# Early token loads on ACT's queue, all four early means on ACT, and a reordered plan, in a fused attention and MLP kernel

## The chip, the core and the metric

The kernel runs on one core of a Trainium2 chip. The core has five engines that run side by side, each with its own queue of instructions: TensorE (PE, matrix products), VectorE (DVE), ScalarE (ACT), GpSimd (POOL) and SyncE (SP, which here only issues transfers). An engine takes its queue in order; a wait at its head holds everything behind it. Transfers between HBM and the on-chip memory SBUF are issued from a queue, here SP's or ACT's, and run on 16 DMA engines. TensorE writes to PSUM, 8 banks of 128 partitions by 2 KB.

The metric is the device time of one execution in microseconds (us), the lower the better. Beside it stands a profile of one execution: when each instruction started, how long it took, and what it waited for.

## What is computed

The input x has 2048 tokens of 640 values. It is normalized by row, and two branches use the result: a linear attention of 32 heads with 20 values each, whose feature map is a softmax of a per-head product and of its negative, and a gated MLP of width 1536. The output is the sum of x and both.

```python
xn = _layernorm(x)                                   # (x - mean) / sqrt(var + 1e-5)
qkv = xn @ wqkv                                      # split to q, k, v: 32 heads x 20
pq = einsum("bhsd,hdf->bhsf", q, w_phi)              # the same for k
phi_q = concatenate([softmax(pq), softmax(-pq)])     # the same for k
kv = einsum("bhsf,bhsd->bhfd", phi_k, v);  z = sum_s phi_k
o = einsum(phi_q, kv) / (einsum(phi_q, z) + 1e-6)
attn = o.reshape(B, S, D) @ wo
mlp = (silu(xn @ w1) * (xn @ w3)) @ w2
return x + attn + mlp
```

All inputs and the output are bf16.

## The kernel before

**Tiles.** The tokens are 16 tiles of 128 (`x_tok[:, t, :]`), the model width 5 chunks of 128, the MLP width 12 chunks. The normalized x is needed transposed (`xnT`), with the width on the partitions, as an operand of every product.

**A planner sets the order.** The kernel is not written as a fixed list. Each operation is recorded with its reads and writes, an engine or a choice of engines, an estimated duration and a level (its priority), and TensorE's work is recorded as units: a group of matmuls with the PSUM banks it needs and the operations that empty them. `_Program.schedule` (L169) then plays the program in a model of the engines: at each step it takes, for each engine, the operation that can start first, or one of a higher level that can start within a small slack, and commits it. The slack for PE units is 0.12 us and for other operations 0.09 us; while the planned time lies below `shaken` it is drawn at random from a short list (PE 0.03 to 0.6 us, others 0.03 to 0.4), from a generator seeded with `SEED`. `emit` (L389) turns the order into one list for each engine, with semaphore waits. So the order of every queue is fixed when the program is built, from the model's times, and the chip then runs each queue in that order with its own times. `late(n, us)` (L584) forbids the operations recorded since n to be planned before a given time.

**Transfers in the plan.** `load` (L641) issues an ordinary transfer, `turn` (L645) a transposing one. In the model all transfers share one line: `commit` adds each one's bytes behind the last, whichever queue it is on.

**The first 24 us.** They run through these names:

- `load_x` (L660) loads token tiles, `load_wv` the value weights `wv` in two parts, `load_wT` (L667) the key weights transposed (`wqkT`), `phi` the small matrices of w_phi (`phi_s`), `load_w13` slices of the MLP weights.
- `ln_stats` (L712): for a tile, two BATCH_NORM_STATS and one aggregation on DVE give mean and variance (`bst`, `mv`); POOL then makes r = (var + eps)^-0.5 with an addition and a power.
- `centre` (L736) makes `xc` = x minus its mean. For a tile marked "ACT" in `CENTRED`, ACT sums the row (`junk`, with an accumulator), and DVE or ACT adds the negative mean; for a tile marked "DVE", DVE subtracts the mean of its own statistics.
- `xc_transpose` (L754; "cT" here) transposes `xc` on PE into PSUM and copies it to `xcT`; `v_first` (L765) multiplies it with `wv` and scales by r while emptying PSUM, so that V of tiles 0 to 3 doesn't wait for the full normalization.
- `ln_apply` (L727) normalizes `x_tok` in place: tiles 0 and 1 on POOL (`POOLED`), tiles 2 and 3 on DVE, the others on DVE or ACT. `xn_transpose` (L779; "xT" here) transposes tiles 0 to 3 on PE into `xnT`; tiles from 4 on are transposed by DMA from SP's queue.
- `block_diag` (L795) makes `BDc`, five products of `phi_s` and a mask `GF` on POOL; its level is 0, the lowest of POOL's early work (normalization 1e5, statistics about 2e5). `fold` (L804) multiplies `wqkT` with `BDc` on PE into `Wkp`, the key weights with the feature matrices folded in. `k_tile` (L859) uses `Wkp` and `xnT`.

After that, PE runs V and K tiles and MLP units (`mlp`, L976) until the sums over all tokens (`kv_sum`, L888) are formed, then the attention units of each token tile (`q_tok`, L934: 20 small matmuls into four banks, two copies by ACT, a chain of small DVE operations, and one product of 1280 elements that frees the banks) between Q and MLP units, and last the output tiles (`out_tile`, L994). While PE has nothing, matmuls of zeros (`filler`, L1019) are put in during the first 12 planned us.

**Who loads what, before.** SP's queue: x tiles 0 and 1, wv chunks 0 and 1, x tiles 2 and 3, five weight transposes, MLP weights and x tiles 8 to 15 and so on. ACT's queue: wv chunks 2 to 4 and phi at the start, x tiles 4 to 7 not before 9 us of plan.

Of the kernel before, what the change touches and what calls it, by code (L numbers as in the profile page):

```python
# [4 lines left out]
ACT = mybir.ActivationFunctionType  # L5
# [27 lines left out]
class _Op:  # L33


    __slots__ = ("ways", "eng", "emit", "raw", "war", "bankd", "succ", "unit", "ismm", "start", "end", "inc", "sem",
                 "clock", "idx", "part", "level", "off", "done", "nbytes", "busy", "left", "name", "deps", "gates", "early", "extra")

    def __init__(self, ways):
        self.ways = ways  # L40
# [26 lines left out]
class _Program:  # L67
# [91 lines left out]
            after = list(after) + [self.unit.mms[-1]]  # L159
        return self.add(o, writes, reads, level, after)  # L160

    def dma(self, eng, emit, writes, reads, nbytes, busy=0.45, level=0.0, after=()):
        o = _Op({eng: (emit, busy, 0.0)})
        o.nbytes = nbytes
        return self.add(o, writes, reads, level, after)


# [1 line left out]
    def schedule(self, start, filler=None, filler_until=0.0, seed=None, shaken=0.0):  # L169
# [12 lines left out]
        for u in self.units:  # L182
            t = 0.0
# [7 lines left out]
            while todo:  # L191
                o = todo.pop()
# [11 lines left out]
                d.gates.append(u)  # L204
        free = dict(start)
        bus = 0.0
        mode = "full"
        owner = [None] * 8
        ready = {e: [] for e in ENGINES}
        ready_u = [u for u in self.units if not u.missing]  # L210
        pool_prev = None
        for o in self.all:
            if not o.ismm and not o.left:
                for e in o.ways:
                    ready[e].append(o)

        def commit(o, e, t):
            nonlocal bus, pool_prev
            o.eng = e
            o.emit, o.busy, dur = o.ways[e]  # L220
            o.start = t
            free[e] = t + o.busy
            if o.nbytes:
                bus = max(bus, t + 0.6) + o.nbytes / 1e3
                o.end = bus + 1.2 + o.extra
            else:
                o.end = t + dur
            o.done = True
            self.ops.append(o)
            if e == "POOL" and not o.nbytes:  # L230
# [63 lines left out]
        left = len(self.all)  # L294
        while left:
            best = None
            pick = None
            if ready_u:
# [4 lines left out]
                for u in ready_u:  # L303
                    extra = MODE if u.mode != mode else 0.0
# [19 lines left out]
            for e in ("ACT", "DVE", "POOL", "SP"):  # L324
                if not ready[e]:
                    continue
                ts = [(max(free[e], op_time(o, e)), o) for o in ready[e]]
                t = min(x[0] for x in ts)
                w = 0.09 if seed is None or t > shaken else rng.choice((0.03, 0.09, 0.09, 0.2, 0.4))
                t, o = min((x for x in ts if x[0] <= t + w), key=lambda x: (-x[1].level, x[1].idx))  # L330
                if len(o.ways) > 1 and o.level > 1.5e6:
                    other = min(max(free[f], op_time(o, f)) + o.ways[f][2] for f in o.ways if f != e)
                    if other < t + o.ways[e][2] - 0.02:
                        ready[e].remove(o)
                        del o.ways[e]
# [7 lines left out]
            t, e, x, k = best  # L343
            if e == "PE":
                t0 = free["PE"]
                if filler is not None and t0 < filler_until and t > t0 + 0.25:
# [3 lines left out]
                    else:  # L350
                        i = None
# [37 lines left out]
    def emit(self, finish):  # L389
# [54 lines left out]
        for o in finish[-4:]:  # L444
            lists["SP"].append(("wait", o.sem[2], o.sem[1]))
        return lists
CENTRED = {0: "ACT", 1: "ACT", 2: "DVE", 3: "DVE"}
POOLED = (0, 1)
SEED = 0
TRIPLES = ((0, 3, 0, 60), (3, 3, 60, 60), (6, 3, 120, 60), (9, 3, 180, 60), (12, 3, 240, 60), (13, 3, 300, 20))  # L450


def bass_parallel_sum__linear_kernel_hedgehog__glu_gated_swiglu__prompt_kernel(
# [13 lines left out]
    P = _Program(nc)  # L467
# [23 lines left out]
    phi_s = new("phi_s", [128, DC, DH], bf)  # L491
# [92 lines left out]
    def late(first, us):  # L584
        for o in P.all[first:]:
            o.early = us

    def sb(*aps):
        return [a for a in aps if hasattr(a, "ap")]
# [42 lines left out]

    queue = {"SP": nc.sync, "ACT": nc.scalar}

    def bus(o, elem):
        n = 1
        for s in o.shape:
            n *= s
        return n * 2 / elem / 16 * max(18.0, 10 + 0.0352 * elem) + 100.0

    def load(o, i, level=0.0, eng="SP", after=()):  # L641
        return P.dma(eng, lambda: queue[eng].dma_start(o, i), sb(o), sb(i), bus(o, 2 * o.shape[-1]), 0.45, level,
                     after)

    def turn(o, i, level=0.0, dram=False):  # L645
        d = P.dma("SP", lambda: nc.sync.dma_start_transpose(o, i), sb(o), sb(i), bus(o, 256),
                  1.31, level)
        d.extra = 1.0 if dram else 0.2
        return d
# [6 lines left out]
    phi_t = A_w_phi.rearrange("h d f -> (h d) f").rearrange("(c p) f -> p c f", p=128)  # L656
# [70 lines left out]
    def ln_apply(t, level):  # L727
        o, m, s, z = x_tok[:, t, :], mv[:, t, 0:1], mv[:, t, 4:5], mv[:, t, 6:7]
        ways = [w_op("DVE", "tensor_scalar", (o, o, m, s, ALU.subtract, ALU.mult), 0.35, 0.44)]
        if t in POOLED:  # L730
            ways = [w_op("POOL", "tensor_scalar", (o, o, m, s, ALU.subtract, ALU.mult), 1.25, 1.3)]
        if t >= 4:
            ways.append(w_act(o, o, ACT.Identity, D, s, z))
        add(ways, [o], [o, m, s, z] if t >= 4 else [o, m, s], None, level)
# [299 lines left out]

    consts()
    lv = 9e5
    load_x(0, 1, lv)
    load_x(1, 2, lv - 1)

    def load_wv(a, b, level, eng):  # L1040
        load(wv[:, a:b, :], wqkv_t[:, a:b, 2 * D:3 * D], level, eng)
    load_wv(0, 2, lv - 2, "SP")
    load_x(2, 3, lv - 3)
    load_wv(2, 5, 2e9, "ACT")
    load_x(3, 4, lv - 4)
    load(phi_s[:], phi_t, 2e9 - 1e3, "ACT")
    for e in range(DC):
        load_wT(1, e, lv - 9 - e)
    load_w13(0, 256, lv - 16)
    n = len(P.all)  # L1050
    load_x(4, 8, 1.9e6, "ACT")
    late(n, 9.0)
    load_w13(256, 512, lv - 20)
    load_x(8, 12, lv - 21)
    load_w13(512, 1024, lv - 22)
# [9 lines left out]
    n = len(P.all)  # L1065
    block_diag(0)
    late(n, 8.0)
    for t in range(4):
        if t in CENTRED:
            centre(t, up - t, CENTRED[t])  # L1070
        ln_apply(t, 1e5 - t)
    for t in range(4):
        if t in CENTRED:
            xc_transpose(t, 6e4 - 10 * t + 15)
        xn_transpose(t, 3e4 - t if t in CENTRED else 6e4 - 10 * t + 15)
    for t in range(4, T, 2):
# [18 lines left out]
    n = len(P.all)  # L1095
# [8 lines left out]
    for b in range(3):  # L1104
        for fc in range(FC):
            n = 12 * b + fc
# [6 lines left out]
    for b in range(NB):  # L1113
        for j in range(4):
            t = 4 * b + j
# [4 lines left out]
    for t in range(T):  # L1120
        out_tile(t, when(200 + 5 * t))

    P.schedule({"PE": 1.25, "ACT": 2.1, "DVE": 0.93, "POOL": 0.8, "SP": 0.81}, filler, 12.0, SEED, 25.0)

    lists = P.emit(finish)

# [58 lines left out]
```

The softmax here doesn't subtract the row's maximum and nothing guards it: scores larger than these inputs give would overflow.

## Time and profile before

| | |
|---|---|
| runs (3) | 276.48, 276.58, 276.74 us; median 276.58 |
| profiled execution | 276.66 us, of which the profile's span is 274.9 |
| PE busy | 266.7 us (97%), 2078 matmuls |
| DVE, ACT, POOL busy | 183.1 (67%), 102.6 (37%), 65.7 us (24%) |
| DMA | 21.98 MB, mean 80 GB/s |
| chain that ended last | PE 91%, POOL 3%, ACT 2%, DVE 1%, waits for issue 1%, DMA 1% |
| TensorE's clock | full (1.00) throughout |

The span reaches from the first to the last recorded instruction. "Chain that ended last" follows the work back from the last instruction, at each step to what released it. A busy share is an average over the whole span; the first 16 us differ from the rest, and they are what most of the change touches.

Landing times of the first transfers, from issue: x tile 0 2.3 us; wv chunks 2 to 4 (480 KB, ACT, issued at 1.26) 4.2 us; wv chunks 0 and 1 (320 KB, SP, issued at 1.73) 5.0 us; phi (ACT, issued at 1.75) 5.2 us; x tiles 4 to 7 (640 KB, ACT, issued at 8.41) 4.9 us; the weight transposes 3.6 to 5.9 us.

### The profile page before, as it was taken

The page shows a single profiled execution, that of the slowest core. Times are in us where ns is not written, and L with a number is a line of the kernel's source. Part 1 is how long each engine was busy: PE and PEld are TensorE (multiplying, and loading weights), DVE is VectorE, ACT ScalarE, POOL GpSimd, SP SyncE. Part 2 cuts the span into 40 slices and gives each one's busy share as a digit, 9 for nine tenths or more (in the row PEclk, how much of TensorE's full clock was granted, in tenths as well). Part 3 has the DMA queues.
Part 4 walks back from the last instruction along what each step waited for, and adds up shares of the span by engine and source line. Part 5 has one row for each costly group of instructions (what it writes and reads, how often), then busy time and mean ns, then how long its engine had stood idle before and what let it go on. Part 6 is the DMA issues. An engine that isn't in the chain of part 4 may idle for free.

```text
span 274.9 us, 5053 instructions
## 1 busy us (share of the span) xinstructions
PE 266.7 (97%) x2078; PEld 158.9 (58%) x2097; DVE 183.1 (67%) x319; ACT 102.6 (37%) x187; POOL 65.7 (24%) x103
## 2 busy tenths in 40 slices
PE   6799999999999999999999999999999999999996
PEld 3575477656654447544444445677777774444774
DVE  4698989999957433678978978577661215666112
ACT  6379377564553451256673382010000002222000
POOL 5923556999997000000000000000000000000000
PEclk9999999999999999999999999999999999999999
DMA  7999997910000000803211111243332222000001
GB/s 216 237 317 347 195 132 129 187 67 0 2 0 2 0 0 2 284 6 27 47 26 24 38 36 24 75 99 95 97 96 75 72 72 74 0 0 0 26 24 48
DMA packets 41255, 21.98 MB, mean 80 GB/s; under 512 B 27024, under 2 KB 41232, under 8 KB 41232
## 3 DMA queue, kind: packets, MB, share of 16 engines
q1 hardware_dynamic: 39648, 20.49, 31.2%
q10 hardware_dynamic: 1584, 1.17, 1.5%
q8 instruction: 16, 0.26, 0.4%
q14 instruction: 7, 0.06, 0.1%
HBM read 12.81 MB, written 2.62 MB: 56 GB/s over the span
## 4 chain that ended last, share of the span: by engine, by line
PE 91%; POOL 3%; ACT 2%; DVE 1%; issue 1%; DMA 1%
PE PS L572 91%; POOL x_tok L580 2%; ACT EqT L580 2%; DMA x_tok<-in_A_x_dram 1%; POOL mv L580 1%; PE PS L787 0%; DVE bst L580 0%; DVE hT L580 0%; DVE den_s L580 0%; DVE xres L580 0%; ACT e_s L580 0%; DVE xc L580 0%; PE PS L757 0%; DVE t L580 0%; DVE pr_s L580 0%
## 5 line engine op out<-in xcount | busy, mean ns | idle before, releaser
L572 PE MATMUL PS<-xnT,w_s 128*128 128x512 bf16 x465 | 105.6, 379 | 1.4 <-issue 0.5
L572 PEld LDWEIGHTS PS<-xnT,w_s 128*128 128x128 bf16 x480 | 46.4, 98 | 54.5 <-DVE hT L580 0.8
L572 PE MATMUL PS<-w_s,hT 128*128 128x320 bf16 x384 | 55.0, 299 | 0.0
L580 ACT ACTIVATE th<-PS 128x512 f32<-128x512 f32 x48 | 28.7, 599 | 66.0 <-PE PS L572 66.0
L580 DVE SCALAR_TENSOR_TENSOR t<-th,PS 128x512 bf16<-128x512 f32 x48 | 32.6, 679 | 24.0 <-ACT th L580 23.9
L572 PEld LDWEIGHTS PS<-w_s,hT 128*128 128x128 bf16 x384 | 37.1, 98 | 14.9
L580 DVE TENSOR_TENSOR xres<-PS,xres 128x640 bf16<-128x640 f32 (+1 forms) x17 | 13.4, 786 | 41.2 <-PE PS L572 41.2
L580 POOL TENSOR_TENSOR ekt<-ekt,rS 128x640 bf16<-128x640 bf16 x32 | 39.6, 1275 | 1.5 <-DVE rS L580 1.5
L580 DVE SCALAR_TENSOR_TENSOR hT<-t,PS 128x512 bf16<-128x512 bf16 x48 | 32.5, 677 | 1.3 <-PE PS L572 0.3
L580 ACT ACTIVATE EqT<-PS 128x512 bf16<-128x512 f32 x40 | 21.9, 594 | 12.6 <-PE PS L572 12.6
L580 DVE TENSOR_REDUCE S<-ekt 128x64 f32<-128x1280 bf16 x16 | 22.9, 1458 | 3.4 <-ACT ekt L580 3.4
L572 PE MATMUL PS<-wo_s,oT 128*128 128x320 bf16 x160 | 24.5, 299 | 0.0
L580 DVE TENSOR_TENSOR prod<-PS,g_s 128x1280 bf16<-128x1280 f32 x16 | 23.8, 1490 | 0.5
L580 ACT ACTIVATE ekt<-PS 128x640 bf16<-128x640 f32 x32 | 20.8, 701 | 8.6 <-PE PS L572 8.4
L572 PE MATMUL PS<-Wkp,xnT 128*128 128x320 bf16 x160 | 23.9, 299 | 0.0
L572 PE MATMUL PS<-xnT,Wqp 128*128 128x512 bf16 x96 | 23.1, 380 | 0.3 <-issue 0.2
L580 ACT ACTIVATE e_s<-PS 128x64 f32<-128x64 f32 x32 | 9.1, 284 | 37.6 <-PE PS L572 37.1
L572 PEld LDWEIGHTS PS<-wo_s,oT 128*128 128x128 bf16 x160 | 15.7, 98 | 6.1
L572 PEld LDWEIGHTS PS<-Wkp,xnT 128*128 128x128 bf16 x160 | 15.5, 98 | 6.0
L572 PE MATMUL PS<-wv,xnT 128*128 128x320 bf16 x120 | 18.3, 299 | 0.0
L580 DVE BATCH_NORM_STATS2 bst<-x_tok 128x6 f32<-128x320 bf16 x32 | 14.3, 469 | 3.0 <-DMA x_tok<-in_A_x_dram 3.0
L572 PEld LDWEIGHTS PS<-xnT,Wqp 128*128 128x128 bf16 x100 | 9.3, 98 | 10.8
(68 smaller groups left out, 172.1 us busy)
## 6 DMA issues: line engine op xcount, KB each, us to landing
w_s<-in_B_w_dram SPq DMA_DIRECT2D x4, 640.0 KB, 9.2
xres<-in_A_x_dram SPq DMA_DIRECT2D x16, 160.0 KB, 2.2
out_dram<-xres SPq DMA_DIRECT2D x15, 160.0 KB, 1.8
w_s<-in_B_w_dram SPq DMA_DIRECT2D x1, 1920.0 KB, 9.2
w_s<-in_B_w_dram SPq DMA_DIRECT2D x4, 320.0 KB, 5.5
x_tok<-in_A_x_dram SPq DMA_DIRECT2D x2, 640.0 KB, 8.4
wo_s<-in_A_wo_dram SPq DMA_DIRECT2D x1, 800.0 KB, 4.9
x_tok<-in_A_x_dram SPq DMA_DIRECT2D x4, 160.0 KB, 4.0
```

What stands on the lines that cost most here:

```text
L572: return nc.tensor.matmul(o(u.k), l, r, start=start, stop=stop, skip_group_check=shared)
L580: return getattr(e, name)(*[at(a, u) for a in args], **{k: at(v, u) for k, v in kw.items()})
```

## The change

- Token tile 0 stays on SP's queue. Tiles 1, 2 and 3 are issued from ACT's queue, not before 1.3, 3.3 and 4.3 us of plan, with a level above ACT's other work but one; tiles 4 to 7 stay on ACT's queue, not before 11.3 instead of 9.0.
- wv is issued from SP in three parts (chunks 0 and 1, 2, 3 and 4), phi from SP after the second weight transpose.
- All four of tiles 0 to 3 get their mean from ACT (`CENTRED`).
- The planner's model of transfers takes turns between the two queues, and lets ACT issue a transfer while its last operation is still running (`issue`).
- `SEED` is 433 instead of 0, the random slack acts until 175 us of plan instead of 25, and ACT's start in the plan is 1.12 instead of 2.1. So the order of units and operations is drawn anew over most of the kernel.

What is computed stays the same, and so do the operations other than the means of tiles 2 and 3.

```diff
@@ schedule
+        issue = {"ACT": start["ACT"]}
+        queues = {"SP": [], "ACT": []}
...
+        def transfer(now):
+            nonlocal bus
+            at = dict.fromkeys(queues, 0)
+            left = {q: [o.nbytes for o in v] for q, v in queues.items()}
...
+                turn = sum(queues[q][at[q]].each for q in go)
+                steps = min(left[q][at[q]] for q in go)
...
         def commit(o, e, t):
...
-            free[e] = t + o.busy
+            free[e] = max(free[e], t + o.busy)
+            if e == "ACT":
+                issue[e] = t + (o.busy if o.nbytes else 0.06)
             if o.nbytes:
-                bus = max(bus, t + 0.6) + o.nbytes / 1e3
-                o.end = bus + 1.2 + o.extra
+                o.begin, o.end = t + 0.6, 1e9
+                queues[e].append(o)
+                transfer(t)
...
-                ts = [(max(free[e], op_time(o, e)), o) for o in ready[e]]
+                ts = [(max(issue[e] if o.nbytes and e == "ACT" else free[e], op_time(o, e)), o) for o in ready[e]]
...
-CENTRED = {0: "ACT", 1: "ACT", 2: "DVE", 3: "DVE"}
+CENTRED = {0: "ACT", 1: "ACT", 2: "ACT", 3: "ACT"}
 POOLED = (0, 1)
-SEED = 0
+SEED = 433
...
+    def on_act(a, b, us):
+        n = len(P.all)
+        load_x(a, b, 2e9, "ACT")
+        late(n, us)
     load_x(0, 1, lv)
-    load_x(1, 2, lv - 1)
+    on_act(1, 2, 1.3)
...
     load_wv(0, 2, lv - 2, "SP")
-    load_x(2, 3, lv - 3)
-    load_wv(2, 5, 2e9, "ACT")
-    load_x(3, 4, lv - 4)
-    load(phi_s[:], phi_t, 2e9 - 1e3, "ACT")
+    load_wv(2, 3, lv - 4, "SP")
+    on_act(2, 3, 3.3)
+    load_wv(3, 5, lv - 5, "SP")
+    on_act(3, 4, 4.3)
     for e in range(DC):
         load_wT(1, e, lv - 9 - e)
+        if e == 1:
+            load(phi_s[:], phi_t, lv - 10.5)
     load_w13(0, 256, lv - 16)
-    n = len(P.all)
-    load_x(4, 8, 1.9e6, "ACT")
-    late(n, 9.0)
+    on_act(4, 8, 11.3)
...
-    P.schedule({"PE": 1.25, "ACT": 2.1, "DVE": 0.93, "POOL": 0.8, "SP": 0.81}, filler, 12.0, SEED, 25.0)
+    P.schedule({"PE": 1.25, "ACT": 1.12, "DVE": 0.93, "POOL": 0.8, "SP": 0.81}, filler, 12.0, SEED, 175.0)
```

More of the change, by code (lines that the diff above doesn't have):

```diff
@@ L36 @@
     __slots__ = ("ways", "eng", "emit", "raw", "war", "bankd", "succ", "unit", "ismm", "start", "end", "inc", "sem",
-                 "clock", "idx", "part", "level", "off", "done", "nbytes", "busy", "left", "name", "deps", "gates", "early", "extra")
+                 "clock", "idx", "part", "level", "off", "done", "nbytes", "busy", "left", "name", "deps", "gates", "early", "extra",
+                 "begin", "each")
     def __init__(self, ways):
@@ L160, in op, with dma @@
         return self.add(o, writes, reads, level, after)
-    def dma(self, eng, emit, writes, reads, nbytes, busy=0.45, level=0.0, after=()):
+    def dma(self, eng, emit, writes, reads, pieces, each, busy=0.45, level=0.0, after=()):
         o = _Op({eng: (emit, busy, 0.0)})
-        o.nbytes = nbytes
+        o.nbytes, o.each = pieces, each
         return self.add(o, writes, reads, level, after)
@@ L215, in schedule @@
                     ready[e].append(o)
+        def transfer(now):
+            nonlocal bus
+            at = dict.fromkeys(queues, 0)
+            left = {q: [o.nbytes for o in v] for q, v in queues.items()}
+            t = 0.0
+            bus = 0.0
+            while True:
+                go, wake = [], 1e9
+                for q, v in queues.items():
+                    if at[q] < len(v):
+                        o = v[at[q]]
+                        if o.begin <= t + 1e-9:
+                            go.append(q)
+                        else:
+                            wake = min(wake, o.begin)
+                if not go:
+                    if wake > 1e8:
+                        break
+                    t = wake
+                    continue
+                turn = sum(queues[q][at[q]].each for q in go)
+                steps = min(left[q][at[q]] for q in go)
+                if wake < t + steps * turn:
+                    steps = (wake - t) / turn
+                t += steps * turn
+                for q in go:
+                    left[q][at[q]] -= steps
+                    if left[q][at[q]] < 1e-6:
+                        o = queues[q][at[q]]
+                        e = t + 1.3 + o.extra
+                        if e > now:
+                            o.end = e
+                        at[q] += 1
+                bus = t
+            for q, v in queues.items():
+                while len(v) > 1 and v[0].end < now - 5.0 and v[1].begin < now - 5.0:
+                    v.pop(0)
         def commit(o, e, t):
-            nonlocal bus, pool_prev
+            nonlocal pool_prev
             o.eng = e
@@ L633, in bass_parallel_sum__linear_kernel_hedgehog__glu_gated_swiglu__prompt_kernel, with pieces @@
     queue = {"SP": nc.sync, "ACT": nc.scalar}
-    def bus(o, elem):
+    def pieces(o, elem):
         n = 1
@@ L638, in bus @@
             n *= s
-        return n * 2 / elem / 16 * max(18.0, 10 + 0.0352 * elem) + 100.0
+        return n * 2 / elem / 16, max(18.0, 10 + 0.0352 * elem) / 1e3
     def load(o, i, level=0.0, eng="SP", after=()):
-        return P.dma(eng, lambda: queue[eng].dma_start(o, i), sb(o), sb(i), bus(o, 2 * o.shape[-1]), 0.45, level,
+        return P.dma(eng, lambda: queue[eng].dma_start(o, i), sb(o), sb(i), *pieces(o, 2 * o.shape[-1]), 0.45, level,
                      after)
     def turn(o, i, level=0.0, dram=False):
-        d = P.dma("SP", lambda: nc.sync.dma_start_transpose(o, i), sb(o), sb(i), bus(o, 256),
+        d = P.dma("SP", lambda: nc.sync.dma_start_transpose(o, i), sb(o), sb(i), *pieces(o, 256),
                   1.31, level)
```

## The prediction

> **What bounds the kernel now.** I read the page's busy shares first, then the chain that ended last, then the timeline of the first 20 us by engine, because the diff touches loads and row means that are all spent by then.
>
> The first view is a table of stretches: from to, length, then busy time and (xcount) of PE, PE's weight loads, DVE, ACT, POOL, then clock, DMA share and GB/s.
>
> ```profile
> 4.00:6.00 2.00, 1.60 (x20) 1.05 (x18) 1.62 (x6) 1.21 (x3) 1.24 (x3) 1.00 1.14 350
> 6.00:8.00 2.00, 1.42 (x14) 0.97 (x12) 0.84 (x4) 0.70 (x1) 2.00 (x1) 1.00 1.18 256
> 8.00:10.00 2.00, 2.00 (x21) 1.54 (x20) 1.90 (x7) 1.03 (x2) 1.92 (x5) 1.00 0.93 188
> 10.00:12.00 2.00, 0.36 (x8) 0.19 (x6) 1.19 (x3) 0.56 (x1) 2.00 (x2) 1.00 1.00 273
> 12.00:14.00 2.00, 2.00 (x22) 1.58 (x23) 1.12 (x3) 0.70 (x1) 2.00 (x5) 1.00 1.18 264
> ```
>
> TensorE loses time in 4 to 12 us and, from 12 us on, hardly any: over the windows from 12 to 250 us I count 1.7 us idle, and most of that is pieces of 0.05 and 0.16 us at which the neighbouring group has 9, 19 or 29 of its 10, 20 or 30 matmuls, so a missing record. The only real wait there is 0.29 us at 144.0 (<-DVE hT). POOL has 2.00 of 2.00 us in three of these windows and 1.92 in the fourth.
>
> The second view is the chain of waits, in order of time:
>
> ```profile
> 4.57 0.25 POOL mv L580
> ...
> 5.74 2.53 POOL x_tok L580
> 8.28 0.22 POOL mv L580
> ...
> 9.36 2.53 POOL x_tok L580
> 11.88 0.05 issue
> 11.93 0.45 PE PS L787 x5
> ...
> 15.94 7.27 PE PS L572 x70
> ```
>
> From 4.57 to 11.88 the end is set by POOL; after that by PE's own row of work.
>
> The third is the timeline (start, duration, engine, line, operation, tiles, count, idle before):
>
> ```profile
> 6.85 2.88 PE L572 MATMUL PS<-wv,xcT 128*128 128x320 bf16 x20 [0.58 <-ACT xcT L580]
> 7.36 0.50 DVE L580 BATCH_NORM_STATS2 bst<-x_tok 128x6 f32<-128x320 bf16 x1 [1.16 <-DMA x_tok<-in_A_x_dram]
> 11.93 0.45 PE L787 MATMUL PS<-ident,x_tok 128*128 128x128 bf16 x5 [1.64 <-POOL x_tok L580]
> 12.82 0.44 DVE L580 TENSOR_SCALAR x_tok<-x_tok,mv 128x640 bf16<-128x640 bf16 x1
> 13.66 1.59 POOL L580 TENSOR_TENSOR BDc<-phi_s,GF 128x140 bf16<-128x140 bf16 x4
> 13.72 1.71 DVE L580 TENSOR_SCALAR x_tok<-x_tok,mv 128x640 bf16<-128x640 bf16 x1 [0.46 <-POOL mv L580]
> 15.21 0.73 PE L787 MATMUL PS<-ident,x_tok 128*128 128x128 bf16 x10
> 15.78 1.87 PE L572 MATMUL PS<-BDc,wqkT 128*128 128x140 bf16 x30
> ```
>
> Read here: V0 and V1 start at 6.85, when wv's first half has just landed (issued at 1.73, 5.0 us to landing); tile 2's statistics wait for its DMA until 7.36; PE's fifth transpose set waits 1.64 us for POOL's second normalization; and the folds of Wkp start at 15.78, half a microsecond after POOL's last product BDc (15.25) and after the two last transposes. All products in BDc must be there before a fold, and K0 needs the folds.
>
> **What the Trainium skill says.** "DMA: Bandwidth & Descriptors", section Issuing engines are not separate DMA queues: transfers from any engine run on the same 16 DMA engines and interleave, so a second issuing engine saves issue time only. Its section Queues, rings and completion order adds that each DMA engine takes turns between queues. The trace agrees so far: x tile 0 took 2.3 us alone, wv's 320 KB behind two tiles and beside ACT's 480 KB took 5.0. "SBUF — State Buffer", section SBUF: two separate sides: VectorE in a two-port mode and GpSimd hold a common port pair exclusively, the later one blocks. The trace agrees: the same normalization took 0.44 us on DVE at 12.82 and 1.71 at 13.72, ending at 15.43, right after POOL's four products.
>
> **The change part by part.**
> Loads. Before, 2 to 4 us moves 254 GB/s (508 KB) and 4 to 6 us 350 GB/s (700 KB), 1.2 MB by 6 us. After, tile 0 is first on SP as before (landed 3.08). ACT issues tile 1 at about 1.26, where it issued wv; it takes turns with wv's first 320 KB. Tiles 0, 1 and that half are 640 KB, through at about 4.35, landed near 4.8: 1.9 us earlier than 6.7. Tile 2 is issued after ACT's first mean (near 3.3 to 3.9), shares with the other 480 KB of wv, and 1280 KB are through by about 6.15: tile 2 lands at 5.5 to 6, the last of wv by 6.6, tile 3 at 6.5 to 7 instead of about 8. An issue takes ACT's queue 0.37 to 0.51 us, but runs beside the operation ahead of it (at 8.41 both start together): three issues cost nothing unless a wait stands ahead of them. On SP two tile loads go (1.18 us) and two pieces of wv and phi come (about 0.45 each), so the five weight transposes of 1.35 us end about where they do, near 10; landing takes up to 5.9, before 15.25.
> Tiles 4 to 7: issue moves from 8.41 to about 11.3 or, behind a V eviction that waits for POOL's r, near 13.7. With 4.9 to 6 us they land at 17 to 19.7; DVE first reads them at 18.19. Behind that read stand statistics whose V4 matmuls start at 33.84, with 10.6 us of MLP work from 23.26 to cover: 0. Without cover it would be 1.5.
> Means. ACT takes tiles 2 and 3: 2 x (0.74 + 0.19) = 1.86 us, in ACT's idle 6.84 to 8.41 and 10.57 to 12.70: 0. The centring of tile 2 can leave DVE near 7.0 rather than 8.83, of tile 3 near 8.3 rather than 9.88.
> PE. V0 starts near 5.9 (xcT0 was ready at 5.79), not 6.85, and V2, V3 no longer need to stand behind the transposes that wait for POOL. All that PE has ahead of the folds is 4 x 1.44 of V and 8 x 0.45 of transposes, 9.4 us; from 4.42, with some 0.5 of waiting early on, it is through near 14.0 instead of 15.8. That is the 1.8 us that the change could bring.
> POOL. Nothing there goes away. From 4.57 it has additions and powers 0.24+0.75, 0.24+0.67, 0.22+0.56, 0.23+0.75 = 3.66, two normalizations 5.06, five products 0.42+1.59 = 2.01: 10.73, which gives 15.30 against 15.25 in the trace. Its start hangs on tile 0 alone, which doesn't move. The products have the lowest level (0 against 1e5 and 2e5), so whatever the order above them, the last one ends at about 15.25. Folds start at 15.3, not 15.78: -0.45. PE then waits about 1.3 us for POOL where it waited for loads. If one transpose of a late tile (0.37, its input blocked until 15.43) is still to do, +0.1 to +0.4 comes back. I take -0.45.
> Order of units. The seed with random slack now acts until 175 us of plan instead of 25. There is 0.3 us of true waiting to win; random slack lets the planner take a PE unit up to 0.6 us late. From -0.3 to +1.2; I take +0.1, as the robust cover of MLP units remains.
> Sum: -0.45 + 0.1 = -0.35. The profiled execution took 276.66 (span 274.9 and 1.76 around it): 276.3; the median of the runs is 0.08 below it: 276.2.
>
> **Rivals.**
> A, the likeliest: POOL takes the place of the loads. 276.2, own range 275.8 to 276.7. For it: POOL without idle from 4.57 to 15.25. Against: the order on POOL is made anew.
> B, POOL's order lets go: with means on ACT and another seed, tile 3's addition and power (0.98) fall behind the products, or are done before the second normalization so that no transpose is left. The products then end at 14.27, folds start 1.5 earlier, 0.37 given back by a late transpose: -1.1, 275.5 (274.8 to 275.9). For it: one product already ran before the last power (12.56). Against: the levels.
> C, slower: the attention units stand closer. A unit of token attention holds four banks from its 20 matmuls until ACT's copies (2 x 0.28), DVE's chain (0.23, 0.20, 0.36, 0.23) and the 1.49 us product are through, about 3.1 us. They start 3.9 to 7.1 us apart between 120 and 166 us. Where two stand under about 3.1 apart, or DVE has three MLP pieces of 0.68 in between, PE waits 0.5 to 0.8. Two such waits, +1.2, give 277.4 (276.9 to 278.2); it decides from a total of 0.9, where it eats A's gain. For it: DVE had 2.83 of 3.00 us at 135 to 138, and the one wait at 144.0. Against: that wait was 0.29.
> D, the change doesn't do what it says: ACT's queue holds tile 2's issue behind the mean until 3.9 and tile 3's behind 5.2; they then land at 6.5 and 7.5. As POOL decides, this is A.
>
> **How the numbers follow.** A (with D) 0.43, B 0.31, C 0.26. 0.2% of 276.58 is 0.55 us, about what a measurement can tell from no change: faster is below 276.03. Of A 0.10 lies below that, 0.31 within, 0.02 above; B is faster; C is slower but for 0.01. Faster 0.41, same 0.32, slower 0.27. The range 275.1 to 277.5 leaves out the low quarter of B and the upper half of C, about 2 in 10.
>
> **What would show it.** V0 at about 5.9, tile 2's statistics no later than 6.5: loads right. POOL dense to about 15.25 and BDc's last product there, PE idle for over 1 us before the folds at 15.3: POOL step right. Folds at 14.5 or earlier: B. Waits <-DVE prod or hT over 1 us in sum between 110 and 200 us: C. I am wrong altogether if POOL idles before 12 us, if its normalizations are not 2.53 us each, or if V4's inputs come late enough to stop PE after 23 us.

## The result and the profile after

The median of four runs after is 278.37 us (277.70 to 279.12), of the kernel before, on the same chip, 276.64 (276.48 to 276.74). The ratio is 1.0064, interval 1.0036 to 1.0091: slower by 1.7 us, where 276.2 was forecast. The profiled execution is the longest of the four: 279.12, span 277.4, so 2.46 us above the profiled execution of before (276.66). Its rows have to explain 2.46; the median has 1.73.

First the timeline of the early loads (start, duration, engine, line, operation, tiles, count, idle before it and what ended that):

```profile
0.81 0.41 ACTq L688 DMA_DIRECT2D x_tok<-in_A_x_dram  x1
...
3.69 0.74 ACT L626 ACTIVATE junk<-x_tok 128x640 bf16<-128x640 bf16 x1 [0.95 <-DMA x_tok<-in_A_x_dram]
...
3.70 0.33 ACTq L688 DMA_DIRECT2D x_tok<-in_A_x_dram  x1
...
9.00 0.74 ACT L626 ACTIVATE junk<-x_tok 128x640 bf16<-128x640 bf16 x1 [2.76 <-DMA x_tok<-in_A_x_dram]
...
10.67 0.74 ACT L626 ACTIVATE junk<-x_tok 128x640 bf16<-128x640 bf16 x1 [0.84 <-DMA x_tok<-in_A_x_dram]
...
12.71 0.39 ACTq L688 DMA_DIRECT2D x_tok<-in_A_x_dram  x1
```

The four `junk` operations are ACT's row means, and three of them show when a tile landed. Tile 0 is there at 3.69, not 3.08: SP issues it at 0.81, and at the same moment ACT issues tile 1, so both share the DMA engines from the start. Tile 2, issued at 3.70, comes 5.2 us later; tile 3, issued at 4.56, lands at 10.6, 6.0 us later. Both come later than before (7.36 and about 8). The last line is the 640 KB of tiles 4 to 7, issued at 12.71 instead of 8.41.

What that does to the DMA engines stands in the table of stretches (busy time and count of PE, weight loads, DVE, ACT, POOL; then clock, DMA share, GB/s):

```profile
8.00:10.00 2.00, 0.90 (x9) 0.39 (x6) 0.64 (x2) 0.83 (x2) 1.81 (x4) 1.00 1.30 189
10.00:12.00 2.00, 1.70 (x15) 1.18 (x15) 1.51 (x4) 1.33 (x4) 2.00 (x1) 1.00 0.84 158
12.00:14.00 2.00, 1.81 (x19) 1.30 (x19) 1.78 (x6) 1.96 (x4) 2.00 (x6) 1.00 0.66 158
```

From 10 to 14 us 158 GB/s are moved where before moved 273 and 264. PE is idle for 1.1 us in 8 to 10, first for POOL (0.56), then for the centring of tile 2 (0.84, into the next stretch). And yet the head of the kernel ends almost where it did:

```profile
9.86 2.70 POOL L626 TENSOR_SCALAR x_tok<-x_tok,mv 128x640 bf16<-128x640 bf16 x1
...
12.73 0.45 PE L833 MATMUL PS<-ident,x_tok 128*128 128x128 bf16 x5
...
13.02 2.88 PE L618 MATMUL PS<-wv,xcT 128*128 128x320 bf16 x20
...
15.52 0.42 POOL L626 TENSOR_TENSOR BDc<-phi_s,GF 128x140 bf16<-128x140 bf16 x1
...
15.74 2.01 PE L618 MATMUL PS<-BDc,wqkT 128*128 128x140 bf16 x30
```

POOL's second normalization ends at 12.56. PE's transposes of tile 1 need it and follow at 12.73; behind them in PE's queue stand V2 and V3 (x20), and behind these, without a gap, the folds at 15.74 (15.78 before). POOL's last product ends at 15.94, 0.20 after the first fold has begun. The first MLP matmul starts at 23.58, 0.32 late. The rest of the loss comes after that, in two lines of PE's timeline:

```profile
23.58 6.64 PE L618 MATMUL PS<-xnT,w_s 128*128 128x512 bf16 x30
...
32.01 1.52 PE L618 MATMUL PS<-wv,xnT 128*128 128x320 bf16 x10 [1.79 <-DVE bst L626]
...
38.02 1.53 PE L618 MATMUL PS<-wv,xnT 128*128 128x320 bf16 x10 [0.42 <-DMA xnT<-x_tok]
```

The same place in the kernel before (one of the 50 matmul records of its five units is missing):

```profile
23.26 10.74 PE L572 MATMUL PS<-xnT,w_s 128*128 128x512 bf16 x49
33.84 1.52 PE L572 MATMUL PS<-wv,xnT 128*128 128x320 bf16 x10
```

V4, the value product of tile 4, now stands behind three MLP units (x30) instead of five, and waits 1.79 us; V6 waits 0.42. The releaser named for the first wait, a DVE statistics operation, is not an input of V4. Its input is the transposing DMA of tile 4, and SP's timeline and the summary of `xnT`'s DMAs give its landing:

```profile
23.25 6.10 SPq L692 DMA_TRANSPOSE xnT<-x_tok  x2
```

```profile
DMA to landing us min/median/max: 2.6/2.7/8.6
```

Issued at 23.25 and up to 8.6 us to landing is 31.85, 0.16 ahead of V4's start. In two runs below in which V4 waits as well the same distance is 0.17 (24.76 + 8.4 against 33.33) and 0.16 (22.82 + 8.1 against 31.08), so I put the wait down to this DMA. Before it was issued at 22.55 and took at most 7.1, so it landed at 29.65 at the latest, and V4 did not come until 33.84:

```profile
22.55 7.64 SPq L646 DMA_TRANSPOSE xnT<-x_tok  x4
```

```profile
DMA to landing us min/median/max: 2.6/3.5/7.1
```

The sum: 0.32 + 1.79 + 0.42 = 2.53, against 2.46. After 38 us PE has no wait worth a line; the chain of waits says the same:

```profile
31.77 6.21 DMA xnT<-x_tok
37.97 0.05 issue
38.02 236.75 PE PS L618 x1859
```

The chain runs through V6's transposing DMA (31.77 to 37.97) and not through V4's. So had V4 alone been served in time, V6 would still have stood until 38.0 in this execution: it is the row of these transposes that is late, not one of them.

### The profile page after: what moved, and what is told of

Its sections match the earlier page's. It is cut to its first block, busy times and chain, and to the rows that moved or that the text cites. A ratio compares the mean times of both kernels' runs of the same rounds, so it can differ in the third digit from the quotient of the medians.

```text
span 277.4 us, 5060 instructions
## 1 busy us (share of the span) xinstructions
PE 269.5 (97%) x2094; PEld 159.2 (57%) x2094; DVE 184.1 (66%) x322; ACT 101.4 (37%) x188; POOL 66.3 (24%) x103
## 4 chain that ended last, share of the span: by engine, by line
PE 89%; DMA 5%; DVE 1%; ACT 1%; SPq 1%; issue 1%; ACTq 0%
PE PS L618 89%; DMA x_tok<-in_A_x_dram 3%; DMA xnT<-x_tok 2%; SPq L692 1%; ACT ekt L626 0%; DVE hT L626 0%; DVE t L626 0%; PE PS L833 0%; DVE bst L626 0%; ACT junk L626 0%; ACT xcT L626 0%; ACT xnT L626 0%; SPq L688 0%; ACT th L626 0%; DVE xres L626 0%
## 5 line engine op out<-in xcount | busy, mean ns | idle before, releaser
L618 PE MATMUL PS<-xnT,w_s 128*128 128x512 bf16 x480 | 107.9, 380 | 0.0
L618 PEld LDWEIGHTS PS<-wv,xnT 128*128 128x128 bf16 x120 | 11.6, 98 | 8.7 <-DVE hT L626 2.3
## 6 DMA issues: line engine op xcount, KB each, us to landing
w_s<-in_B_w_dram SPq DMA_DIRECT2D x4, 640.0 KB, 10.6
```

What stands on the lines that cost most here:

```text
L618: return nc.tensor.matmul(o(u.k), l, r, start=start, stop=stop, skip_group_check=shared)
```

## The experiments

The question has two halves. Why does V4 wait: is its transpose late, or is V4 planned too early, and what made the plan so? And why does the head gain nothing although all the loads were rearranged for it?

Where a kernel keeps the order of another ("orders kept"), its planned lists are taken and only the named operations are moved, with this helper ahead of `emit`:

```python
acts = [o for o in P.ops if o.eng == "ACT"]
lds = [o for o in acts if o.nbytes]          # ACT's transfers
comp = [o for o in acts if not o.nbytes]     # ACT's operations
def put(o, prev):
    P.ops.remove(o)
    P.ops.insert(P.ops.index(prev) + 1, o)
```

### Tiles 4 to 7 issued early again

After's orders kept; the load of tiles 4 to 7 goes out behind ACT's mean of tile 2.

```diff
+    put(lds[3], comp[4])
```

> The changed kernel with every queue's order kept, except that ACT issues x tiles 4 to 7 right behind its mean of tile 2 (near 9.0 us instead of 12.71). Theory S (starved DMA: the rings ran at 158 GB/s from 10 to 14 us against 268 before, so all that is queued behind, up to the transposes of tile 4 that V4 waits for, is late): 10 to 14 us back above 230 GB/s, the transpose of tile 4 lands 1 us or more earlier than 31.9, PE's wait before V4 (1.8) falls below 0.8, time 277.2 or less. Rival T (the statistics of tile 4 on DVE start at 19.16 whatever the load does, and they set the transpose): the wait stays within 0.4 of 1.8, time 278.0 to 278.8.

Measured: 276.98 (276.74 to 278.73), ratio to before 1.0019 (1.001 to 1.0029). One DMA moved by 4.3 us takes back 1.4 of the 1.7. The table of stretches and PE's timeline of this kernel:

```profile
10.00:12.00 2.00, 1.70 (x17) 1.09 (x14) 1.32 (x4) 1.73 (x4) 2.00 (x1) 1.00 1.12 333
12.00:14.00 2.00, 1.80 (x20) 1.31 (x18) 1.39 (x5) 1.57 (x3) 2.00 (x6) 1.00 1.17 298
```

```profile
23.36 6.64 PE L618 MATMUL PS<-xnT,w_s 128*128 128x512 bf16 x30
...
29.83 1.52 PE L618 MATMUL PS<-wv,xnT 128*128 128x320 bf16 x10
```

With the load at 8.46 the stretch from 10 to 14 us moves 333 and 298 GB/s instead of 158, tile 4's transpose is issued at 22.84 and lands at 29.64 at the latest (6.8 us), and V4 starts without a wait, behind the same three MLP units. S held, T fell. It has next to nothing in hand: V4 starts 0.19 after that landing, and where it waited it started 0.16 or 0.17 after. Two of the three executions above 277.5 (277.88 and 278.73) have a mean clock of 0.994, the third (278.40) 0.999; no trace of them is kept, so whether V4 waits in them is not shown.

### V4 behind one more MLP unit

Tiles 4 to 7 stay late; V4 and K4 may not be planned ahead of the fourth MLP unit, and the plan is made anew with this one rule.

```diff
+    named = {u.name: u for u in P.units}
+    for n in ("V4", "K4"):
+        named[n].behind.append(named["M0.3"].mms[-1])
```

> The changed kernel with V4 and K4 held in the plan until a fourth MLP unit (2.16 us of matmuls); head and loads as they are. Theory O (the order of units: three MLP units instead of five stand before V4, so PE arrives 2.2 us too early): no wait before V4 nor V6, time 276.0 to 276.6, about the time of before. Rival L (the load chain is later in the whole, tiles 5 to 7 as well): the wait moves to V5 or V6, and the time stays above 277.5.

Measured: 276.94 (276.66 to 281.72), ratio 1.0024 (1.001 to 1.0039). By the time, the other half of the pair is enough by itself too: with one more unit of cover, 0.3 us are left over the kernel before. O's time was missed by 0.3 us above the upper end of its band; L's (above 277.5) fell. That V4's wait is gone was not seen, as the only trace is of the longest execution of the twenty (281.72), far from the median.

### The planner keeps its backlog

After's new transfer model (`transfer` in `schedule`) plays the queues of SP and ACT again from the start at each step, and drops a transfer that ended over 5 us ago if the next one was issued as long ago. What was dropped no longer holds up what was issued after it, so the model forgets a queue's backlog. Here only the dropping is gone, and the whole plan is made anew.

```diff
-            for q, v in queues.items():
-                while len(v) > 1 and v[0].end < now - 5.0 and v[1].begin < now - 5.0:
-                    v.pop(0)
```

> The changed kernel with the model's three lines left out that drop finished transfers from its queues (after that it replays the rest from their issue times, as if nothing stood ahead of them). Theory M (the model forgets its backlog and so believes in early transposes): the plan itself puts a fourth MLP unit before V4, PE's wait there is gone, time as in a2_one_more_mlp within 0.3, 276.0 to 276.6. Rival N (the model's dropping is harmless, and the early V4 is the seed's doing): time within 0.4 of 278.4.

Measured: 276.35 (276.13 to 278.89), ratio 1.0001 (0.9983 to 1.0019).

```profile
23.34 8.80 PE L615 MATMUL PS<-xnT,w_s 128*128 128x512 bf16 x40
...
31.97 1.52 PE L615 MATMUL PS<-wv,xnT 128*128 128x320 bf16 x10
```

The plan puts four units (x40) ahead of V4, which starts at 31.97 without a wait, although tiles 4 to 7 are still issued at 12.55 and their first transpose at 22.96. M held in its order and its time, though the time is 0.6 below that of one more unit, where 0.3 was expected: without the three lines the loss is gone. As the plan is a new one, other places of it differ too; that cover ahead of V4 is enough is shown by the second experiment. The backlog is not a cure for every plan, as the last experiment shows.

### The late load in the kernel before

Before's orders kept; its load of tiles 4 to 7 goes behind ACT's copy of `xcT` of tile 3, issued at 12.66.

```diff
+    put(lds[2], comp[7])
```

> The kernel before with every queue's order kept, except that ACT issues x tiles 4 to 7 behind its copy of xcT of tile 3 (near 12.7 us, as in the changed kernel, instead of 8.41). Theory C (the five MLP units before V4 are the cover; the load's lateness alone costs nothing): the transpose of tile 4 lands 1 to 2.5 us later, V4 starts without a wait at 33.8, time within 0.3 of before. Rival D (the late load is the loss in itself): 277.6 or more.

Measured: 277.30 (276.60 to 279.10), ratio 1.0035 (1.0023 to 1.0047), between the two theories. The profiled execution is the shortest of the twenty, 276.6. In it V4 starts at 33.80 without a wait; the transpose of tile 4, issued at 23.85 and at most 6.1 on its way, has landed by 29.95, only 0.3 later than before and not the 1 to 2.5 expected. So five MLP units cover the late load in that execution, and the 0.7 us of the median were not seen in any trace. What they are stays open.

### The old seed in the new kernel, the new one in the old

```diff
-SEED = 433
+SEED = 0
...
-..., filler, 12.0, SEED, 175.0)
+..., filler, 12.0, SEED, 25.0)
```

> The changed kernel (its loads, means and model of transfers) with the seed and the reach of the random slack of before (0, 25 us). Theory M (the model, not the seed, puts V4 behind three MLP units): three units again, PE waits 1.2 to 3 us before V4, time 277.5 to 279. Rival N (the seed did it): no wait before V4, time 276.0 to 276.8.

Measured: 282.42 (280.04 to 282.83), ratio 1.0191 (1.0148 to 1.0234). V4 again stands behind three units, and waits 2.12 us, so the seed isn't what moved it: M held in the order and the wait. The time is far above both bands. The timeline, and the stretches around it:

```profile
24.56 6.64 PE L618 MATMUL PS<-xnT,w_s 128*128 128x512 bf16 x30
...
33.33 1.82 PE L618 MATMUL PS<-wv,xnT 128*128 128x320 bf16 x10 [2.12 <-DVE bst L626]
```

```profile
32.50:35.00 2.50, 1.68 (x11) 1.17 (x12) 2.43 (x9) 0.00 (x0) 1.29 (x4) 0.88 1.30 177
35.00:40.00 5.00, 5.00 (x28) 3.17 (x27) 4.49 (x12) 2.73 (x5) 3.54 (x16) 0.72 0.77 112
40.00:45.00 5.00, 5.00 (x39) 3.61 (x37) 4.05 (x6) 4.98 (x8) 4.08 (x13) 1.00 0.83 132
```

About 1.1 us after the wait ends, TensorE's granted clock falls. The table gives means of stretches (0.88 and 0.72); in finer ones it is 0.50 from 34.4 to 37.8 and 1.00 on both sides. V4's ten matmuls take 1.82 us instead of 1.52. The sum over before: MLP 1.30 later (24.56 against 23.26), the wait 2.12, the clock 2.5 x 0.12 + 5 x 0.28 = 1.7; 5.1 of the 5.5 us between the profiled executions. Three of the four runs have a mean clock of 0.993 or 0.994 (282.15 to 282.83); the fourth, at 1.00, took 280.04.

The other way round, in the kernel before:

```diff
-SEED = 0
+SEED = 433
...
-..., filler, 12.0, SEED, 25.0)
+..., filler, 12.0, SEED, 175.0)
```

> The kernel before (its loads, means and model) with the seed and reach of the change (433, 175 us): the order of units drawn anew, alone. Theory M: five MLP units before V4, no wait there, time within 0.6 of before. Rival N: 277.6 or more.

Measured: 277.49 (277.36 to 277.61), ratio 1.0031 (1.0019 to 1.0043), 0.3 us beyond M's band. V4 stands behind five units and has no wait. The MLP starts at 22.42, 0.84 earlier than before, although POOL's last product ends at 15.17 (15.25 before): in this plan V2 and V3 stand ahead of the transposes that wait for POOL. The gain is lost later, and more:

```profile
22.42 10.96 PE L572 MATMUL PS<-xnT,w_s 128*128 128x512 bf16 x50
33.21 1.52 PE L572 MATMUL PS<-wv,xnT 128*128 128x320 bf16 x10
```

```profile
PE PS L572 <- DVE hT L580: 1.1, 2, 0.6
```

The two waits, 1.1 us at 144 and 155, meet the sign that rival C had named; before has 0.29 there. That is 0.8 of the 1.6 us lost after 22.42, and another wait, at 64.88, has 0.27; the rest was not located. In the changed kernel that mechanism is absent: no waits after 38 us.

So the seed doesn't move V4: with either one the kernel before has five MLP units ahead of it and the changed kernel three. Taking out the dropping makes three into four, in the plan above that keeps the backlog and in the last experiment. What takes away the fifth, the new loads or the rest of the new model, was not separated.

### Tiles 2 and 3 at once

After's orders kept; ACT issues tiles 2 and 3 straight behind tile 1.

```diff
+    put(lds[1], lds[0])
+    put(lds[2], lds[1])
```

> The changed kernel with every queue's order kept, except that ACT issues x tiles 2 and 3 right behind tile 1, by 1.7 us instead of 3.70 and 4.56. Theory Q (behind the wv parts and the weight transposes of SP's ring a transfer on ACT's ring is held back): tile 2 lands by 6 us instead of 8.9, tile 3 by 7 instead of 10.6, PE's 3.1 us of waiting between 8 and 13 us shrink by more than 1.5. Theory P (POOL's 10.7 us from the first statistics on hold the folds): folds start no earlier than 15.2 all the same, and the time falls by less than 0.6. Rival F (the loads alone hold the head): folds start by 14.3, and the time falls by 1.2 or more.

Measured: 278.08 (277.81 to 278.43), ratio 1.0055 (1.0039 to 1.0072). The timeline:

```profile
5.90 0.73 ACT L626 ACTIVATE junk<-x_tok 128x640 bf16<-128x640 bf16 x1
...
6.90 0.74 ACT L626 ACTIVATE junk<-x_tok 128x640 bf16<-128x640 bf16 x1 [0.18 <-DMA x_tok<-in_A_x_dram]
...
15.28 0.42 POOL L626 TENSOR_TENSOR BDc<-phi_s,GF 128x140 bf16<-128x140 bf16 x1
...
15.46 2.06 PE L618 MATMUL PS<-BDc,wqkT 128*128 128x140 bf16 x30
```

Tile 2 is there by 5.90 and tile 3 at 6.9, some 3 and 3.8 us sooner than in the changed kernel and as early as the forecast had put them. The folds begin 0.28 sooner. V4 still waits (1.09, and V6 0.29); the load of tiles 4 to 7 moved along, to 11.36. P held and F fell. Q held for the landings only: PE's idle time from 8 to 13 us, which was to shrink by more than 1.5, is 1.82 us against 1.59 in the changed kernel (the 3.1 of the expectation isn't in its trace). PE only waits at another place, for POOL's second normalization, which ends at 12.32: so its idle time ahead of the late loads was a symptom.

### All loads early, and a normalization taken from POOL

The first kernel takes the one with the backlog kept and moves both loads early; the second also gives DVE the normalization of tile 1, which was POOL's.

```diff
+    put(lds[1], lds[0])
+    put(lds[2], lds[1])
+    put(lds[3], comp[5])
```

> a3_backlog_kept with its orders, tiles 2 and 3 issued right behind tile 1, and tiles 4 to 7 right behind ACT's mean of tile 3 (near 7.5). Theory P (POOL holds the folds): folds at 15.2 to 15.6, no wait after 20 us, time 276.0 to 276.6, though tiles 2 and 3 land 2.5 us or more earlier than in a3_backlog_kept. Rival F (loads hold the head): folds by 14.5, 275.4 or less.

```diff
+    y = [o for o in P.ops if o.eng == "POOL"][11]
+    y.eng = "DVE"
+    y.emit = lambda: nc.vector.tensor_scalar(x_tok[:, 1, :], x_tok[:, 1, :], mv[:, 1, 0:1], mv[:, 1, 4:5],
+                                             ALU.subtract, ALU.mult)
+    put(y, [o for o in P.ops if o.eng == "DVE" and o is not y][17])
```

> d1_all_early with one operation moved: the normalization of tile 1 on DVE (0.44 us there) instead of POOL (2.53). Theory P: POOL's last product ends near 12.8 to 13.3, folds start at 14.2 to 14.9, time 0.6 to 1.3 below d1_all_early: 275.0 to 275.8. Rival F: POOL isn't what holds the folds, so folds stay at 15.2 or later and the time within 0.3 of d1_all_early.

Measured: all early 276.48 (276.34 to 276.84), ratio 0.9995 (0.9987 to 1.0004); with the normalization on DVE 274.87 (274.87 to 274.97), ratio 0.9936 (0.992 to 0.9953). Early loads alone are worth nothing, as P said. The folds of the first kernel and of the second:

```profile
15.34 0.43 POOL L623 TENSOR_TENSOR BDc<-phi_s,GF 128x140 bf16<-128x140 bf16 x1
...
15.53 2.06 PE L615 MATMUL PS<-BDc,wqkT 128*128 128x140 bf16 x30
```

```profile
13.43 0.42 POOL L623 TENSOR_TENSOR BDc<-phi_s,GF 128x140 bf16<-128x140 bf16 x1
...
14.16 1.89 PE L615 MATMUL PS<-BDc,wqkT 128*128 128x140 bf16 x30
```

POOL's last product ends at 13.85 instead of 15.77, the folds begin 1.37 earlier (14.16 against 15.53), and the time falls by 1.61. P held in its direction, with sizes beside its bands: the product was expected by 13.3, the gain at 1.3 at most. PE's transposes of tile 1 move from 12.53 to 11.16. In the first kernel the profile puts their wait down to a copy of `xcT` by ACT; POOL's normalization, which is their input, had ended at 12.39, and as the second kernel runs them before the same copy, the copy was not what held them. This kernel beats both, before by 1.7 us.

The same move in the kernel before, by the places of its own lists:

```diff
+    y = [o for o in P.ops if o.eng == "POOL"][12]
...
+    put(y, [o for o in P.ops if o.eng == "DVE" and o is not y][18])
```

> The kernel before with one operation moved: the normalization of tile 1 on DVE behind the centring of tile 3, instead of POOL; all other orders kept. Theory P (POOL bounds the head of the kernel before too): PE's 1.64 us of waiting for it at 10.3 falls below 0.6, POOL's last product ends by 13.2, folds start by 14.9 instead of 15.78, time 275.2 to 276.0. Rival F (the late loads of tiles 2 and 3 bound it): folds at 15.4 or later, time within 0.3 of before.

Measured: 275.38 (275.32 to 275.61), ratio 0.9956 (0.9939 to 0.9972). Its timeline:

```profile
10.83 0.45 PE L787 MATMUL PS<-ident,x_tok 128*128 128x128 bf16 x5 [0.27 <-DVE x_tok L1133]
...
11.55 1.75 POOL L580 TENSOR_TENSOR BDc<-phi_s,GF 128x140 bf16<-128x140 bf16 x4
...
14.68 1.76 PE L572 MATMUL PS<-BDc,wqkT 128*128 128x140 bf16 x30
```

The 1.64 us that PE waited at 11.93 for POOL become 0.27 at 10.83, the folds begin 1.10 earlier, the time falls by 1.2. P held, but for POOL's last product, which ends at 13.30 and not by 13.2: POOL bounded the head before the change as well. With this normalization gone, the chain of waits begins with the load of tile 2 (2.20 to 7.49), so here a load is next in line.

### Tile 0 without company

The kernel at 274.87, with all of ACT's first loads behind its warming activation, so that tile 0 has the DMA engines to itself until 1.26.

```diff
+    put(lds[0], comp[0])
     put(lds[1], lds[0])
```

> d2_norm1_on_dve with ACT's first three loads behind its first small activation, so that they are issued at 1.26 and not at 0.81 together with tile 0's. If tile 0's later landing (3.69 against 3.08) comes from sharing with tile 1, it lands at 3.0 to 3.2, all the head moves up by 0.4 to 0.5, folds 13.8 to 14.5, time 0.3 to 0.6 below d2_norm1_on_dve. If it comes from something else, tile 0 still lands after 3.4 and the time is within 0.2.

Measured: 274.96 (274.76 to 275.95), ratio 0.9945 (0.9925 to 0.9966).

```profile
3.10 0.74 ACT L623 ACTIVATE junk<-x_tok 128x640 bf16<-128x640 bf16 x1 [0.79 <-DMA x_tok<-in_A_x_dram]
...
5.36 0.74 ACT L623 ACTIVATE junk<-x_tok 128x640 bf16<-128x640 bf16 x1 [1.43 <-DMA x_tok<-in_A_x_dram]
```

Tile 0 lands at 3.10 again, so the company was what delayed it, and POOL starts at 4.55. Tile 1 pays, at 5.36, and POOL then waits for `phi` until 10.02. The folds begin at 14.06, within the band, but only 0.10 sooner than without the edit, and the expected 0.3 to 0.6 did not come: the time is the same. The chain of waits now begins with the load of tile 1 (1.26 to 5.27).

### A plan without normalizations on POOL

Backlog kept, tiles 1 to 3 at 1.3 us of plan, tiles 4 to 7 at 9.0, and everything planned anew with

```diff
-POOLED = (0, 1)
+POOLED = ()
```

> A version planned anew: the model keeps its backlog, tiles 1 to 3 issued at once, tiles 4 to 7 from 9 us of plan, and no normalization on POOL. POOL's work before the folds falls by 5.06 us to about 5.7. Theory P then has PE's own work as the bound: folds at 13.0 to 14.2, time 274.3 to 275.2, at or a little below d2_norm1_on_dve (274.87). If DVE, which takes both normalizations, becomes the bound, the folds start after 14.4 and the time is 275.2 or more.

Measured: 279.21 (277.83 to 280.21), ratio 1.0089 (1.0054 to 1.0125), a miss of both bands. The timeline and one stretch:

```profile
13.55 0.42 PE L615 MATMUL PS<-BDc,wqkT 128*128 128x140 bf16 x5
15.62 1.63 PE L615 MATMUL PS<-BDc,wqkT 128*128 128x140 bf16 x25 [1.66 <-DMA wqkT<-in_A_wqkv_dram]
...
23.08 8.80 PE L615 MATMUL PS<-xnT,w_s 128*128 128x512 bf16 x40
34.17 2.41 PE L615 MATMUL PS<-wv,xnT 128*128 128x320 bf16 x10 [2.29 <-DMA xnT<-x_tok]
```

```profile
35.00:40.00 5.00, 5.00 (x27) 3.17 (x26) 0.82 (x3) 1.95 (x4) 1.84 (x10) 0.69 0.81 117
```

The folds begin at 13.55, as expected, but wait 1.66 us for a weight transpose. Then V4, behind four MLP units, waits 2.29 for its own, and again the clock falls behind that wait (0.50 from 34.6 to 38.1, the mean of the stretch 0.69). With POOL out of the way the transposing loads are the next limit in this plan, and even with the backlog in it the plan's model of transfers is too hopeful for them.

## Why the prediction was wrong

**Tiles 4 to 7: the step that failed.** "10.6 us of MLP work from 23.26 to cover: 0. Without cover it would be 1.5." Issue (12.71 against "about 11.3 or [...] 13.7") and landing (12.71 + 6.4 = 19.1, within 17 to 19.7) came as forecast. The cover did not stay: it belonged to the old plan, and the new one left 6.64 us, three units, from 23.58. V4 and V6 waited 2.21 us in the profiled execution. The prediction had the price of the uncovered case, 1.5 to be held against these 2.21, and none of its rivals used it; its last sentence named the sign ("if V4's inputs come late enough to stop PE after 23 us"). Either remedy alone, the early load or one more unit, brings 1.4 us back. What placed V4 early is the new transfer model, which forgets backlog: it puts three units ahead of V4 with either seed, and four without the dropping, where the loss is gone (the fifth was not traced to a cause). The full difference of the two kernels has those lines, though the excerpt above leaves them out. The prediction priced the moved loads and the seed, but not that the model which sets every order had changed.

**Loads.** Tile 0 "doesn't move" was wrong by 0.61 (3.69 against 3.08): ACT issues tile 1 at 0.81, not 1.26, as the transfer stands ahead of ACT's first activation; behind it, in the run with tile 0 alone, it goes out at 1.26. "DMA: Bandwidth & Descriptors", Queues, rings and completion order, in the Trainium skill had been used for the two queues' turns; it applies to tile 0 as well, and the run with tile 0 alone (3.10) agrees. Tile 2 at "5.5 to 6" was 8.94, tile 3 at "6.5 to 7" was 10.6. V0, forecast at 5.9, began at 6.78, and "tile 2's statistics no later than 6.5" failed with it. SP's queue loses three tile loads and not two, and yet its five weight transposes ended at 11.37 and not "near 10".

**POOL and PE: the size right, the path not.** 10.73 us of chain were summed; from 5.14 to 15.94 it is 10.80. The folds, forecast at 15.3, began at 15.74, as the start was 0.57 later. So the 0.45 was eaten by tile 0's lateness. But the sign named for this step, PE idle for over 1 us before the folds, did not show. V2 and V3 did still stand behind the transposes that wait for POOL, and PE ran them right up to the folds; nor must all of `BDc` be there before the folds begin, as they began 0.20 before POOL's last product ended. POOL holds the folds by two ways, its second normalization by way of PE's queue and its last product, and that they come out within 0.2 us of each other is luck for the forecast. PE's own sum has a slip as well: 4.42 + 9.4 + 0.5 is 14.3, not "near 14.0", so it promised 1.5 and not 1.8. That POOL, and not the landing of tiles 2 and 3, sets the end of the head is shown three times: by early tiles that bring 0.28, and by one normalization less on POOL, which brings 1.6 and 1.2. The 0.32 at 23.58 is of the size of the return that the text allowed for (0.1 to 0.4), with two transposes and not one: ten matmuls, 0.56 us, now stand behind the folds, at 17.75.

**Means.** No cost was seen, as forecast: ACT's waits ahead of them end with the tiles' landing.

**Order of units.** +0.1, rival C and its 26 in 100 looked at 110 to 200 us; PE has no wait there in the changed kernel. Rival B (POOL lets go) did not come about by the change; moving one normalization brought what it had named, folds near 14.3 and a time near 275.5, by another way.

Rivals A and D said that POOL leaves the loads little to bring, and for the head that is so. The forecast's fault was to take the calm after 23 us as a property of the kernel, where it was one of the plan.

## What to carry to other kernels

When a planner or its cost model is part of a change, every slack of the old schedule is up for reckoning again: price each wait also without its cover, and give the uncovered case its own rival. An engine idle in front of late loads doesn't make the loads the bound; look for the engine that is dense through the whole stretch and take work off it. In a model of shared queues, a transfer that has ended must still be counted when those behind it are timed.

## What the runs showed of the hardware

- **A short wait of TensorE can cost twice.** In three executions the granted clock fell to 0.50 for 3.4 us, some 1.7 us of time on top: after a wait of 2.12 us (old seed, 34.4 to 37.8), after one of 2.29 (no normalization on POOL, 34.6 to 38.1), and in the long execution with one more MLP unit after two waits of 1.16 and 1.50 with 0.44 of matmuls between (10.8 to 14.2). After the 1.79 us wait of the changed kernel it stayed at 1.00, and so it did in the old seed's head, after waits of 1.27 and 1.16 with 0.45 between. "TensorE: Matmul & The Clock Gate", What's actually happening, in the Trainium skill speaks of an idle window of about 3.4 us; in these three traces less idle time was enough, and by these five cases the length of the wait alone doesn't decide. Whether the wait is the cause wasn't tried by itself.
- **A small load on a quiet queue is not quick.** Tile 2's 160 KB took 5.2 us when issued at 3.70, beside `wv` and weight transposes on SP's queue; issued at 1.24 it was there by 5.90. Tile 0's took 2.9 beside one other tile and 2.3 alone.
- **A DMA in front of ACT's first activation holds up the load of its function table** (ACT_TABLE_LOAD): with one in front it starts at 1.24, with three at 2.25, with none at 0.80.
- **The spread of runs differs, and a wait seen on a DMA doesn't explain it.** Four runs of the changed kernel cover 1.4 us, four of the one before 0.26, four of the fastest one 0.1. But kernels whose trace shows no wait at V4 spread as well: 2.0 us with tiles 4 to 7 early (20 runs), 2.8 with the backlog kept (12), 2.5 with the late load in the kernel before (20), against 0.5 with all loads early (12). The reason is open.
